# Linear attention and a gated feed-forward layer on one core: h split ahead of six splits, two sums a step sooner, casts a step later

## The chip, the cores and the metric

The kernel runs on one core of one Trainium2 chip. The metric is the device time in microseconds (us) of an execution, given as the median of several runs. The engines are named as the profile names them: PE is TensorE's matmuls and PEld its weight loads, DVE is VectorE, ACT ScalarE, POOL GpSimd and SP SyncE.

## What is computed

An attention without a score matrix is followed by a gated feed-forward layer (8 sequences of 576 tokens, 8 heads of 64; 4608 tokens of 512, 1536 hidden):

```python
q_s = softmax(q, axis=-1)               # over the 64 of a head
k_s = softmax(k, axis=2)                # over the 576 tokens
kv = np.einsum('bhsd,bhse->bhde', k_s, v)
x = np.einsum('bhsd,bhde->bhse', q_s, kv)   # then to 4608 x 512
gate = 1.0 / (1.0 + np.exp(-(x @ w_gate)))
return (gate * (x @ w_val)) @ w_out
```

## The kernel before

The tokens are worked through in nine windows of 512 (w = 0 to 8). Window 0 goes another way, in which the weights are also read and prepared; it ends some 180 us into the span. Each window from 1 on has six steps, `at` = 0 to 5, one for each pair of blocks of 128 hidden columns.

A step of window w is one call of `g1` and one of `g2`. `g1` makes gate and value of a pair of blocks by a Strassen scheme: seven products of 12 matmuls each (line 655), from c_hl (the activations, split into a rounded high part and the difference, fp32r) and the split weights a_w and s_sb. The first, third, fifth and seventh product go to the PSUM tile y, the second and sixth to z, the fourth to rr. The third accumulates onto the first, so `nc.scalar.copy(out=sg[:, 0], in_=y)` (line 673) has to read the first product before. Copies and additions (lines 675 to 687) combine them in sg, sigmoids (688, 691, 692) and multiplications (694 to 696) make the hidden values there. `h_split` (lines 705 and 706) splits these into h_hi and h_lo on VectorE, which reads sg for the last time. `g2` multiplies h of the step before with the output weights into acc (line 723, 24 matmuls); in a window's step 0 it is the last step of the window before, and `acc_out` copies acc to x_32 on ScalarE (line 629) and sends it out.

Beside window w the attention of window w + 1 is prepared, in pieces that `side_a` and `side_b` issue after `g1` and `g2` of a step:

- step 0: row maxima of q are taken and sent, q and two tiles of k have their maxima subtracted
- step 1: the rest of k, the exponentials of q and k (lines 457, 357), and the sums of exponentials of k^T (`k_sum`, line 313: an ACTIVATE with an accumulator on a kT tile, 128 x 576) for the third and fourth pair of heads
- step 2: the k-v products (`k_mm`, line 378); the subtraction on qT; `k_done`, which scales the k-v products into kmax_b (line 388) and, in `kv_split`, casts them to kv_sb on ScalarE (line 412) and takes the difference on VectorE (line 413)
- step 3: exponentials of qT; `k_sum` for the first two pairs of heads of the sequence after
- step 4: split of qT, the products with kv_sb that make x (`x_mm`, line 538), copies to x_32, and `c_subs`, the differences of activations that the next window's scheme needs
- step 5: ahead of h, the seven splits of `c_split` (casts on ScalarE, line 594; differences on VectorE, line 595); loads for the window after the next

Sequences exist for windows 2 to 7 only, so `k_sum`, `k_mm` and `k_done` run beside windows 1 to 6. The order on each engine is the order in which the code issues (a manual schedule): each engine works through its own list, and an instruction that waits holds what stands behind it.

Of the kernel before, what the change touches and what calls it, by code (L numbers as in the profile page):

```python
# [51 lines left out]
def attn_moe(ctx: ExitStack, tc: tile.TileContext, qf, qn, qT, k, kT, v, wg, wv, wo, out):  # L52
# [32 lines left out]
    kv_0 = f_last[:, 0].rearrange("p n (h e) -> p (n h) e", e=P)  # L85
# [225 lines left out]
    def k_sum(b, hp):  # L311
        t = kT_sb.pop((b, hp))
        nc.scalar.activation(
            t, t, AF.Exp, bias=kneg[b][:, hp:hp + 1], accum_out=ksum[b][:, hp:hp + 1]
        )
# [33 lines left out]
    def k_sub(b, t, eng=nc.vector):  # L349
        n = KTILES[t][1]  # L350
        kt = kt_sb[b, t]
        eng.tensor_tensor(out=kt[:n], in0=kt[:n], in1=kmb[b][:n], op=ALU.subtract)

    def k_exp(b, t):
        n = KTILES[t][1]
        kt = kt_sb[b, t]
        nc.scalar.activation(kt[:n], kt[:n], AF.Exp)
# [26 lines left out]
    def diag_put(o, ps, k_r, h0, h1):  # L384

        for a in range(2):
            sl = slice(a * D, (a + 1) * D)
            nc.vector.tensor_tensor(  # L388
                out=o(sl), in0=ps[sl, :, sl],
                in1=k_r[sl, h0:h1].unsqueeze(2).broadcast_to([D, h1 - h0, D]), op=ALU.mult,  # L390
            )
# [8 lines left out]
    def k_done(b):  # L400
        k_r = ksum.pop(b)
        nc.vector.tensor_scalar_add(k_r, k_r, EPS)
        nc.vector.reciprocal(k_r, k_r)
        kv = kmax_b[:, 0:NP * D].rearrange("p (h e) -> p h e", e=D)
        diag_put(lambda sl: kv[sl], kvps.pop(b), k_r, 0, NP)
        kv_split(b, lambda sl: kv[sl])

    def kv_split(b, kv):
        hi, lo = (kv_sb[:, b % 2, i] for i in range(2))
        for a in range(2):  # L410
            sl = slice(a * D, (a + 1) * D)
            nc.scalar.copy(out=hi[sl, :, sl], in_=kv(sl))  # L412
            nc.vector.tensor_tensor(
                out=lo[sl, :, sl], in0=kv(sl), in1=hi[sl, :, sl].bitcast(F32), op=ALU.subtract
            )
# [19 lines left out]
    def qn_send(w, what):  # L435
        t = (q_m if what == "m" else q_r)[w]
        row = dpool.tile([H * T], F32, name=f"q_{what}_row")
        nc.sync.dma_start(
            out=row.rearrange("(p i) -> p i", p=P), in_=t.rearrange("p i one -> p (i one)")
        )  # L440
        q_row[w, what] = row.rearrange("(h t) -> h t", t=T)

    def qn_max(w, c):
        if c == 0:
            q_m[w] = const.tile([P, NC * TI, 1], F32, name="q_m")
        nc.vector.tensor_reduce(
            out=q_m[w][:, c * TI:(c + 1) * TI], in_=qn_sb[w, c], axis=AX.X, op=ALU.max
        )

    def qn_sub(w, c, eng=nc.vector):  # L450
        t = qn_sb[w, c]
        m = q_m[w][:, c * TI:(c + 1) * TI]
        eng.tensor_tensor(out=t, in0=t, in1=m.broadcast_to([P, TI, D]), op=ALU.subtract)

    def qn_exp(w, c):
        t = qn_sb[w, c]
        nc.scalar.activation(t, t, AF.Exp)

    def qn_sum(w, c):
        t = qn_sb[w, c]  # L460
        if c == 0:
            q_r[w] = const.tile([P, NC * TI, 1], F32, name="q_r")
        nc.vector.tensor_reduce(
            out=q_r[w][:, c * TI:(c + 1) * TI], in_=t, axis=AX.X, op=ALU.add
        )
        if c == NC - 1:
            t = q_r[w]
            nc.vector.tensor_scalar_add(t, t, EPS)
            nc.vector.reciprocal(t, t)
            if w >= NF:  # L470
                qn_send(w, "r")
# [15 lines left out]
    def qT_sub(w, hp, eng=nc.vector):  # L487
        t = qT_sb[w, hp]
        eng.tensor_tensor(out=t, in0=t, in1=q_b.pop((w, "m", hp)), op=ALU.subtract)
# [12 lines left out]
    def qT_exp(w, hp):  # L502
        t = qT_sb[w, hp]
        nc.scalar.activation(t, t, AF.Exp)
# [65 lines left out]
    def quarter(kh, th):  # L570
        return x_32[:, 2 * kh:2 * kh + 2, th * HT:(th + 1) * HT]
# [15 lines left out]
    def c_split(i):  # L587
        if i % 2 == 0:
            t = cpool.tile([P, 2 if i < 6 else 1, 2, 2, HT], F32R, name="c_hl", tag=f"c{i // 2}")
            for x in range(i, min(i + 2, 7)):  # L590
                c_hl[x] = t[:, x % 2]
        src = c_32.pop(i) if i in c_32 else quarter(*{B11: (0, 0), B21: (1, 0), B22: (1, 1)}[i])
        hi, lo = (c_hl[i][:, x] for x in range(2))
        nc.scalar.copy(out=hi, in_=src)
        nc.vector.tensor_tensor(out=lo, in0=src, in1=hi.bitcast(F32), op=ALU.subtract)
# [104 lines left out]
    def h_split(w, p):  # L700
        h_hl[w, p] = hi, lo = [
            two.tile([P, 2, T], F32R, name="h", tag=f"h_{x}") for x in ("hi", "lo")
        ]
        hi, lo = (t.rearrange("p i (q t) -> p (i q) t", q=2) for t in (hi, lo))
        nc.vector.tensor_copy(out=hi, in_=sg[:, :, 0])
        nc.vector.tensor_tensor(  # L706
            out=lo, in0=sg[:, :, 0], in1=hi.bitcast(F32), op=ALU.subtract
        )
# [24 lines left out]
    def side_a(n, p):  # L733

        b = n if n < B else None
        if p == 0:
            for c in range(NC):
                qn_max(n, c)
            qn_send(n, "m")
            for c in range(NC):  # L740
                qn_sub(n, c)
            if b is not None:
                k_sub(b, 0); k_sub(b, 1)
        if p == 1:
            if b is not None:
                for t in range(2, 5):
                    k_sub(b, t)
            for c in range(NC):
                qn_exp(n, c)
            if b is not None:  # L750
                for t in range(5):
                    k_exp(b, t)
                k_sum(b, 2); k_sum(b, 3)
            for c in range(NC):
                qn_sum(n, c)
        if p == 2:
            if b is not None:
                for t in range(5):
                    k_mm(b, t)
            for hp in range(NP):  # L760
                qT_sub(n, hp)
            if b is not None:
                k_done(b)
        if p == 3:
            for hp in range(NP):
                qT_exp(n, hp)
        if p == 4:
            for hp in range(NP):
                qT_split(n, hp)
# [49 lines left out]
    def beside_first(j):  # L819
        if j == 6:  # L820
            k_done(1)
        if 7 <= j <= 10:
            x_ev(1, j - 7)
        if 6 <= j <= 9:
            qT_split(1, j - 6)
# [180 lines left out]
    for j in range(NJ):  # L1006
        g1_0(j)
        beside_first(j)
        split = splits.get(j)
        if split is not None:  # L1010
            split_hi(split)
        if j > 0:
            wo_hi(j - 1)
        if j + 2 < NJ:
            w_top(j + 2)
        if j + 1 < NJ:
            w_join(j + 1)
            wo_top(j + 1)
        wo_join(j)
        if j > 0:  # L1020
            g_mul_0(j - 1)
        if j + 3 < NJ:
            w_low(j + 3)
        if j + 2 < NJ:
            wo_low(j + 2)
        g_sig_0(j)
        if j > 0:
            wo_save(j - 1)
        if j + 3 < NJ:
            load_wo(j + 3)  # L1030
        if j + 5 < NJ - 1:
            load_w(j + 5)
        if j == 7:
            load_w(NJ - 1)
        if split is not None:
            split_lo(split)
        if j + 1 in splits:
            w_sums(splits[j + 1])
        if j > 0:
            g2_0(j - 1)  # L1040
        if j == 3:
            kv_split(0, lambda sl: kv_0[sl, :, sl])
        after_first(j)

    wo_hi(NJ - 1)
# [9 lines left out]
    for w in range(1, NW):  # L1055
        last = w == NW - 1
        for at in range(NS):
            p = step(w, at)
            end = last and at == NS - 1
            g1(w, p, None if end else step(w + (at + 1) // NS, (at + 1) % NS))  # L1060
            if at == NS - 1 and not last:
                for i in range(7):
                    c_split(i)
            h_split(w, p)
            if not last:
                side_a(w + 1, at)
            if prev is None:
                g2_0(NJ - 1)
                wo_next(1, 0)
                wo_next(1, 1)  # L1070
            else:
                g2(*prev)
                if not end:
                    wo_next(w + (at + 1) // NS, (at + 1) % NS)
            prev = (w, at)
            if not last:
                side_b(w + 1, at)
# [39 lines left out]
```

## Time and profile before

| | before |
|---|---|
| median of 3 runs | 982.61 us (979.5 to 984.96) |
| span of the profiled execution | 984.2 us, mean TensorE clock 0.985 of full speed |
| busy: PE, PEld | 954.0 us (97%), 824.0 us (84%) |
| busy: DVE, ACT, POOL | 613.1 us (62%), 471.4 us (48%), 167.3 us (17%) |
| mean share of the DMA engines, bytes | 262 GB/s, 257.78 MB |
| chain of work that ended last | PE 66%, DMA 17%, DVE 7%, ACT 7% |

The profiled execution lies inside the range of the runs, 1.6 us above their median. Busy time of an engine is summed over the whole span; what a step waits for is read from the timeline of that step. The clock is below full speed only in the first slices of the span.

### The profile page before, as it was taken

How to read it: one execution, taken by the hardware profiler on the slowest of the kernel's cores; microseconds unless marked ns; L12 is line 12 of the kernel's file. 1: busy time of each engine (PE TensorE's matmuls, PEld its weight loads, DVE VectorE, ACT ScalarE, POOL GpSimd, SP SyncE). 2: the span in 40 equal slices, each digit the busy share in tenths (PEclk: the TensorE clock that was granted, in tenths of full speed). 3: DMA queues.
4: the chain of work that ended last, by engine and by line, in shares of the span. 5: the costliest groups of instructions: out<-in, count | busy, mean ns of one | idle time of the engine just before them, and what ended most of it. 6: DMA issues, size and time to landing. Idle time of an engine off the chain costs nothing.

```text
span 984.2 us, 15634 instructions
## 1 busy us (share of the span) xinstructions
PE 954.0 (97%) x6062; PEld 824.0 (84%) x6062; DVE 613.1 (62%) x1013; ACT 471.4 (48%) x812; POOL 167.3 (17%) x316
## 2 busy tenths in 40 slices
PE   5899999799999999999999999999999999999998
PEld 5544544599999999999989999899999999999997
DVE  8688778776666566755684667557654655463242
ACT  4589785553436354525362545353434434533222
POOL 0110001221122112111111111121112121212210
PEclk7899999899999999999999999999999999999999
DMA  9987484899699978998899869996998779858662
GB/s 337 330 244 267 165 291 166 302 350 323 203 245 361 306 229 212 374 284 259 180 381 304 261 143 375 332 276 132 374 317 239 216 237 312 248 176 251 199 206 74
DMA packets 93864, 257.78 MB, mean 262 GB/s; under 512 B 15264, under 2 KB 17568, under 8 KB 93024
## 3 DMA queue, kind: packets, MB, share of 16 engines
q0 software_dynamic: 43712, 168.32, 56.9%
q1 hardware_dynamic: 50080, 88.48, 30.6%
q8 instruction: 48, 0.79, 0.4%
q14 instruction: 24, 0.20, 0.1%
HBM read 228.20 MB, written 28.56 MB: 261 GB/s over the span
## 4 chain that ended last, share of the span: by engine, by line
PE 66%; DMA 17%; DVE 7%; ACT 7%; issue 2%; SPq 1%; POOL 0%; DVEq 0%; ACTq 0%; POOLq 0%
PE gv L655 37%; PE acc L723 19%; DMA ring<-k_in 3%; DMA q_m_row<-q_m 3%; PE gv L610 3%; DMA q_b<-q_m_row 3%; DMA kmax_row<-k_max 2%; PE gv L538 2%; DMA ring<-qT_in 1%; PE at L378 1%; PE acc L637 1%; DMA ring<-qn_in 1%; DMA s<-s_sb 1%; DMA wo<-wo_hl 1%; PE at L538 1%
## 5 line engine op out<-in xcount | busy, mean ns | idle before, releaser
L655 PE MATMUL gv<-c_hl,s_sb 128*128 128x256 f32 x2304 | 288.1, 280 | 4.3 <-ACT sg L673 4.2
L655 PEld LDWEIGHTS gv<-c_hl,s_sb 128*128 128x128 f32 x2304 | 276.7, 188 | 6.9 <-ACT sg L673 6.5
L723 PE MATMUL acc<-wo_hl,h 128*128 128x512 f32 x1152 | 272.2, 392 | 0.0
L723 PEld LDWEIGHTS acc<-wo_hl,h 128*128 128x128 f32 x1152 | 213.1, 188 | 44.3
L655 PE MATMUL gv<-c_hl,a_w 128*128 128x256 f32 x1728 | 226.1, 279 | 0.7 <-DVE a_w L269 0.7
L655 PEld LDWEIGHTS gv<-c_hl,a_w 128*128 128x128 f32 x1728 | 214.9, 188 | 5.2 <-issue 1.0
L278 POOL DMA_DIRECT2D s_sb<-s x188 | 100.1, 532 | 321.8 <-PE gv L655 317.5
L681 DVE TENSOR_TENSOR sg<-gv,sg 128x512 f32<-128x512 f32 x48 | 33.2, 691 | 163.0 <-PE gv L655 163.0
L234 POOL DMA_DIRECT2D wo_hl<-wo x96 | 50.9, 531 | 297.6 <-PE acc L723 295.4
L683 ACT COPY sg<-gv 128x512 f32<-128x512 f32 x48 | 28.1, 586 | 106.4 <-PE gv L655 106.4
L610 PE MATMUL gv<-x,f_w 128*128 128x512 f32 x160 | 72.4, 606 | 5.5 <-ACT h L618 5.5
L673 ACT COPY sg<-gv 128x512 f32<-128x512 f32 x48 | 28.0, 583 | 89.8 <-PE gv L655 65.1
L685 DVE TENSOR_TENSOR sg<-sg 128x512 f32<-128x512 f32 x48 | 33.2, 692 | 58.9 <-ACT sg L683 58.9
L610 PEld LDWEIGHTS gv<-x,f_w 128*128 128x128 f32 x160 | 30.5, 194 | 43.7 <-issue 36.0
L706 DVE TENSOR_TENSOR h<-sg,h 128x1024 fp32r<-128x1024 f32 x48 | 58.8, 1226 | 1.6
L688 ACT ACTIVATE sg<-sg 128x512 f32<-128x512 f32 x48 | 30.3, 632 | 55.8 <-DVE sg L687 55.8
L694 DVE TENSOR_TENSOR sg<-sg 128x512 f32<-128x512 f32 x48 | 33.2, 693 | 33.5 <-ACT sg L688 33.5
L637 PE MATMUL acc<-wo_t,h 128*128 128x512 f32 x96 | 45.3, 617 | 5.7 <-DVE h L622 5.6
L678 ACT COPY sg<-gv 128x512 f32<-128x512 f32 x48 | 28.1, 586 | 44.7 <-PE gv L655 44.7
L637 PEld LDWEIGHTS acc<-wo_t,h 128*128 128x128 f32 x96 | 18.8, 199 | 30.0 <-issue 21.7
L675 ACT COPY sg<-gv 128x512 f32<-128x512 f32 x48 | 28.1, 586 | 26.2 <-PE gv L655 26.1
L412 ACT CAST kv_sb<-kmax_b 64x256 fp32r<-64x256 f32 x14 | 5.7, 404 | 67.1 <-DVE kmax_b L388 66.8
(152 smaller groups left out, 1054.8 us busy)
## 6 DMA issues: line engine op xcount, KB each, us to landing
s_sb<-s POOLq DMA_DIRECT2D x188, 512.0 KB, 7.6
wo_hl<-wo POOLq DMA_DIRECT2D x96, 512.0 KB, 6.0
s<-s_sb POOLq DMA_DIRECT2D x6, 2048.0 KB, 7.6
out<-x SPq DMA_DIRECT2D x36, 256.0 KB, 9.6
ring<-k_in SPq DMA_DIRECT2D x28, 256.0 KB, 15.0
ring<-qn_in SPq DMA_DIRECT2D x28, 256.0 KB, 10.3
q_b<-q_m_row SPq DMA_DIRECT2D x56, 128.0 KB, 8.6
ring<-qT_in SPq DMA_DIRECT2D x28, 256.0 KB, 8.9
```

The costliest lines, as they stand in the source:

```text
L234: nc.gpsimd.dma_start(out=t.rearrange("p h e -> p (h e)"), in_=wo_dram[2 * p + i].bitcast(F32R))
L278: nc.gpsimd.dma_start(out=s_sb[:, i].rearrange("p h n e -> p (h n e)"), in_=s_dram[p][:, i * n:(i + 1) * n].bitcast(F32R),)
L538: nc.tensor.matmul(ps[:, f:t], lhsT=kl if lh else kh, rhs=rh[:, f:t], start=(lh == 0 and rh is qh), stop=(lh == 1),)
L610: nc.tensor.matmul(ps[n], lhsT=w[:, kt // 2, sl], rhs=x_0[:, kt], start=(kt == 0), stop=(kt == NK - 1),)
L637: nc.tensor.matmul(acc[0][m], lhsT=h_0[j][:, m * P:(m + 1) * P], rhs=wo_t[j // 2][:, j % 2], start=(j == 0), stop=(j == NJ - 1),)
L655: nc.tensor.matmul(ps[:, n], lhsT=lh(kt), rhs=c_hl[i][:, x, kt], start=(first and n == 0 and kt == 0 and lh is wh and x == 0), stop=(last ...
L681: nc.vector.tensor_tensor(out=sg[:, 0], in0=rr, in1=sg[:, 0], op=ALU.add)
L685: nc.vector.tensor_tensor(out=sg[:, 3], in0=sg[:, 3], in1=sg[:, 2], op=ALU.add)
L688: nc.scalar.activation(sg[:, 0:2, 0], sg[:, 0:2, 0], AF.Sigmoid)
L694: tt(out=sg[:, 0:2, 0], in0=sg[:, 0:2, 0], in1=sg[:, 0:2, 1], op=ALU.mult)
L706: nc.vector.tensor_tensor(out=lo, in0=sg[:, :, 0], in1=hi.bitcast(F32), op=ALU.subtract)
L723: nc.tensor.matmul(acc[w][m], lhsT=h[lh][:, i, sl], rhs=o[i][:, rh], start=(at == 0 and i == 0 and lh == 0 and rh == 0), stop=(at == NS - ...
```

## The change

Three pieces of work are issued elsewhere; nothing is added to or taken from the computation, and no DMA changes its place on its queue.

- At the end of a window, `c_split(0)` stays first, then comes `h_split`, then the other six `c_split`.
- The two `k_sum` of step 1 are issued in step 0, after its subtractions.
- `kv_split` leaves `k_done` (step 2) and is issued at the start of step 3. In window 0 both stay together where they were.

```diff
         diag_put(lambda sl: kv[sl], kvps.pop(b), k_r, 0, NP)
-        kv_split(b, lambda sl: kv[sl])
-
-    def kv_split(b, kv):
+        kv_32[b] = lambda sl: kv[sl]
+
+    kv_32 = {}
+
+    def kv_split(b):
+        kv = kv_32.pop(b)
...
                 k_sub(b, 0); k_sub(b, 1)
+                k_sum(b, 2); k_sum(b, 3)
         if p == 1:
...
                 for t in range(5):
                     k_exp(b, t)
-                k_sum(b, 2); k_sum(b, 3)
...
         if p == 3:
+            if b is not None:
+                kv_split(b)
             for hp in range(NP):
                 qT_exp(n, hp)
...
             if at == NS - 1 and not last:
-                for i in range(7):
+                c_split(0)
+                h_split(w, p)
+                for i in range(1, 7):
                     c_split(i)
-            h_split(w, p)
+            else:
+                h_split(w, p)
```

The lists of the engines show the three moves. Line numbers of the changed kernel are 3 higher from line 413 on.

ScalarE, window 1, from the last sigmoids of step 0 to the first copy of step 1, in the kernel before (sg holds the products of g1, kt_106 and kt_107 are the kT tiles, x_101 is x_32):

```order
L691 ACTIVATE sg<-sg 128x256
L692 ACTIVATE sg<-gv 128x256
L629 COPY x_101<-acc 128x512 x4
L673 COPY sg<-gv 128x512
L675 COPY sg<-gv 128x512
```

The same stretch of this engine in the changed kernel:

```order
L694 ACTIVATE sg<-sg 128x256
L695 ACTIVATE sg<-gv 128x256
L313 ACT_TABLE_LOAD
L313 ACTIVATE kt_106,k_sum<-kt_106,k_neg 128x576
L313 ACTIVATE kt_107,k_sum<-kt_107,k_neg 128x576
L632 COPY x_101<-acc 128x512 x4
L676 COPY sg<-gv 128x512
L678 COPY sg<-gv 128x512
```

A table load and the two sums now stand ahead of the copies of acc.

ScalarE, from the end of step 1 of window 1 to the first copy of step 2, and on to the first table load of step 2, in the kernel before:

```order
L457 ACT_TABLE_LOAD
L457 ACTIVATE ring<-ring 128x512 x4
L357 ACTIVATE ring<-ring 128x512 x4
L357 ACTIVATE ring<-ring 64x512
L313 ACTIVATE kt_106,k_sum<-kt_106,k_neg 128x576
L313 ACTIVATE kt_107,k_sum<-kt_107,k_neg 128x576
L673 COPY sg<-gv 128x512
L675 COPY sg<-gv 128x512
L678 COPY sg<-gv 128x512
L683 COPY sg<-gv 128x512
L688 ACT_TABLE_LOAD
```

The same stretch of this engine in the changed kernel:

```order
L691 ACT_TABLE_LOAD
L691 ACTIVATE sg<-sg 128x2x256
L694 ACTIVATE sg<-sg 128x256
L695 ACTIVATE sg<-gv 128x256
L460 ACT_TABLE_LOAD
L460 ACTIVATE ring<-ring 128x512 x4
L357 ACTIVATE ring<-ring 128x512 x4
L357 ACTIVATE ring<-ring 64x512
L676 COPY sg<-gv 128x512
```

The copy follows the nine exponentials directly, and step 1's sigmoids have a table load of their own ahead of them. The list of ScalarE grows by 12 table loads over the program.

VectorE, from the last multiplication of a window's step 5 (window 1) to the first addition of the next window, in the kernel before (c_hl are the split activations, h the split hidden values):

```order
L696 TENSOR_TENSOR sg<-gv,sg 128x256
L595 TENSOR_TENSOR c_hl<-x_101,c_hl 128x512
L595 TENSOR_TENSOR c_hl<-ring,c_hl 128x512 x2
L595 TENSOR_TENSOR c_hl<-x_101,c_hl 128x512
L595 TENSOR_TENSOR c_hl<-ring,c_hl 128x512
L595 TENSOR_TENSOR c_hl<-x_101,c_hl 128x512
L595 TENSOR_TENSOR c_hl<-ring,c_hl 128x512
L705 CAST h<-sg 128x1024
L706 TENSOR_TENSOR h<-sg,h 128x1024
L681 TENSOR_TENSOR sg<-gv,sg 128x512
```

The same stretch of this engine in the changed kernel:

```order
L699 TENSOR_TENSOR sg<-gv,sg 128x256
L598 TENSOR_TENSOR c_hl<-x_101,c_hl 128x512
L708 CAST h<-sg 128x1024
L709 TENSOR_TENSOR h<-sg,h 128x1024
L598 TENSOR_TENSOR c_hl<-ring,c_hl 128x512 x2
L598 TENSOR_TENSOR c_hl<-x_101,c_hl 128x512
L598 TENSOR_TENSOR c_hl<-ring,c_hl 128x512
L598 TENSOR_TENSOR c_hl<-x_101,c_hl 128x512
L598 TENSOR_TENSOR c_hl<-ring,c_hl 128x512
L684 TENSOR_TENSOR sg<-gv,sg 128x512
```

The two instructions of h stand ahead of six of the seven differences.

## Rows read from the trace of the kernel before

In the rows of a timeline stand the start in us from the start of the span, the duration in us, engine, line, operation, out<-in, shapes and the count of merged instructions; in brackets the idle time before, and what ended it.

**Rows 1.** The page's first part, TensorE's busy time, share of the span, and instructions
```profile
PE 954.0 (97%) x6062; PEld 824.0 (84%) x6062; DVE 613.1 (62%) x1013; ACT 471.4 (48%) x812; POOL 167.3 (17%) x316
```

**Rows 2.** Waits of PE: releaser, us in all, times, longest
```profile
PE gv L655 <- ACT sg L673: 4.2, 9, 0.6
```

**Rows 3.** Timeline of PE, step 2 of window 2: start, us, [idle <- releaser]
```profile
312.14 1.52 PE L655 MATMUL gv<-c_hl,a_w 128*128 128x256 f32 x12
313.50 1.52 PE L655 MATMUL gv<-c_hl,s_sb 128*128 128x256 f32 x12
315.58 1.68 PE L655 MATMUL gv<-c_hl,s_sb 128*128 128x256 f32 x12 [0.55 <-ACT sg L673]
317.10 1.57 PE L655 MATMUL gv<-c_hl,a_w 128*128 128x256 f32 x12
318.51 2.99 PE L655 MATMUL gv<-c_hl,s_sb 128*128 128x256 f32 x24
```

**Rows 4.** Timeline of ACT, the same stretch
```profile
307.44 1.28 ACT L457 ACT_TABLE_LOAD   x1
308.74 2.20 ACT L457 ACTIVATE ring<-ring 128x512 f32<-128x512 f32 x4
...
313.45 0.76 ACT L313 ACTIVATE kt<-kt,k_neg 128x576 f32<-128x576 f32 x1
...
314.97 0.56 ACT L673 COPY sg<-gv 128x512 f32<-128x512 f32 x1
```

**Rows 5.** Timelines of ACT and of PE, step 3 of window 6
```profile
738.80 0.86 ACT L412 CAST kv_sb<-kmax_b 64x256 fp32r<-64x256 f32 x2 [11.74 <-DVE kmax_b L388]
...
740.33 1.68 PE L655 MATMUL gv<-c_hl,s_sb 128*128 128x256 f32 x12 [0.63 <-ACT sg L673]
```

**Rows 6.** Timelines of DVE and ACT, from window 3 to window 4
```profile
482.59 0.68 DVE L595 TENSOR_TENSOR c_hl<-ring,c_hl 128x512 fp32r<-128x512 f32 x1
483.19 0.68 DVE L705 CAST h<-sg 128x1024 fp32r<-128x1024 f32 x1
483.90 1.23 DVE L706 TENSOR_TENSOR h<-sg,h 128x1024 fp32r<-128x1024 f32 x1
...
485.22 0.58 ACT L673 COPY sg<-gv 128x512 f32<-128x512 f32 x1 [3.34 <-DVE h L706]
```

**Rows 7.** Timeline of PE, second and third product of step 0, windows 2, 8
```profile
283.02 3.34 PE L655 MATMUL gv<-c_hl,s_sb 128*128 128x256 f32 x24
...
883.76 3.12 PE L655 MATMUL gv<-c_hl,s_sb 128*128 128x256 f32 x24
```

**Rows 8.** Windows: busy us per engine (instructions), TensorE clock, DMA share, GB/s
```profile
753.00:762.52 9.52, 9.52 (x85) 9.51 (x84) 2.51 (x4) 4.05 (x6) 2.65 (x5) 1.00 0.72 215
802.67:812.56 9.89, 9.89 (x85) 9.89 (x84) 4.88 (x8) 3.52 (x7) 2.64 (x5) 1.00 0.97 297
```

**Rows 9.** Timeline of ACT, step 0 of window 2 and what follows
```profile
292.05 0.37 ACT L692 ACTIVATE sg<-gv 128x256 f32<-128x256 f32 x1
295.27 2.65 ACT L629 COPY x<-acc 128x512 f32<-128x512 f32 x4 [2.86 <-PE acc L723]
298.69 0.58 ACT L673 COPY sg<-gv 128x512 f32<-128x512 f32 x1 [0.77 <-PE gv L655]
```

**Rows 10.** Timeline of ACT, step 0 of window 1 and what follows
```profile
193.30 0.36 ACT L692 ACTIVATE sg<-gv 128x256 f32<-128x256 f32 x1
...
197.99 0.58 ACT L673 COPY sg<-gv 128x512 f32<-128x512 f32 x1 [0.83 <-PE gv L655]
```

**Rows 11.** Timeline of PE, second and third product of step 1, window 1
```profile
197.79 2.99 PE L655 MATMUL gv<-c_hl,s_sb 128*128 128x256 f32 x24
```

**Rows 12.** Timeline of ACT, sigmoid behind a table load, window 1, step 2
```profile
221.90 0.63 ACT L688 ACTIVATE sg<-sg 128x512 f32<-128x512 f32 x1 [0.33 <-DVE sg L687]
```

**Rows 13.** Timeline of ACT, step 4 of window 1
```profile
249.34 0.58 ACT L673 COPY sg<-gv 128x512 f32<-128x512 f32 x1 [1.26 <-PE gv L655]
```

**Rows 14.** Timeline of DVE, step 5 of window 1: k_neg written
```profile
271.25 0.15 DVE L307 TENSOR_SCALAR k_neg<-k_max 128x1 f32<-128x1 f32 x1
```

More of the change, by code (lines that the diff above doesn't have):

```diff
@@ L821, in beside_first @@
             k_done(1)
+            kv_split(1)
         if 7 <= j <= 10:
@@ L1041, in attn_moe @@
         if j == 3:
-            kv_split(0, lambda sl: kv_0[sl, :, sl])
+            kv_32[0] = lambda sl: kv_0[sl, :, sl]
+            kv_split(0)
         after_first(j)
```

## The prediction, made before the changed kernel ran

> **What bounds the kernel now.** I read the page's engine shares first: TensorE is busy 97% of the span [rows 1], so only what lets its matmuls start sooner or follow each other more closely can shorten it. The view of waits, for TensorE alone, comes next: from 206 us on the one thing it is seen to wait for is the ScalarE copy of line 673, nine times, 4.2 us in all [rows 2]. That copy moves the first product of a gate-value block from PSUM to sg, and the third product may not begin before it, as it accumulates into the same PSUM tile. The timelines then say why the copy is late. There are three places; I number a window's six steps 0 to 5, as the code's `at` does.
>
> Step 2, six windows (w 1 to 6). The reader should see that the products start 1.36 us apart (312.14, 313.50), while the third starts only at 315.58: 0.72 us late. Restarting costs a little more: that product takes 1.52 us up to the next, where the one behind it takes 1.41. So a wait shown as 0.55 us of idle costs 0.83, which is 0.28 more than its idle time [rows 3]. ScalarE was at work without a break: table load, nine exponentials, the two sums of exponentials of line 313 (313.45 to 314.97), and only then the copy [rows 4]. The two sums are 1.52 us of it.
>
> Step 3. ScalarE stands 11.74 us at the cast of line 412, until VectorE has written kmax_b; the copy queued behind it then holds TensorE for 0.63 us [rows 5]. This is the longest of three such waits.
>
> Step 0, seven windows. VectorE finishes its seven splits of c_hl, and only then the two halves of h; the copy of line 673 overwrites sg, which the second half reads, and so stands idle for 3.34 us [rows 6]. For TensorE this is nearly covered: two products that take 2.99 us undisturbed [rows 3] take 3.34 at 283.02 and 3.12 at 883.76, the first and the last of seven, most of them 0.11 to 0.13 long [rows 7]. These are too short to be listed as waits.
>
> Beside waits there is a pace. Two steps with no idle time, both at a granted clock of 1.00, which is 2.4 GHz, take 9.52 and 9.89 us for the same 84 matmuls, and TensorE's weight loads cover both without a gap [rows 8]. Some 12 of the 48 steps, counting parts, have the short spacing. In the PE timeline it holds until something interrupts it, the products of x always leave the long one behind, and it returns mostly in the step after a wait.
>
> **The change, part by part.** *Sums a step sooner.* Two ACTIVATEs leave step 1's chain and stand in step 0, between that step's last sigmoid and the four copies of acc. In step 2 the copy of line 673 can then start 1.52 us sooner by ScalarE's queue, where 0.72 is wanted; it now waits for its own product instead. All six waits go; they are priced below with the three of step 3.
>
> What it adds: sigmoids follow in step 1, so there is one table load for the exponentials and one back for the sigmoids, 12 more in all. In step 0 the sigmoid of line 692 ends at 292.42, the load takes 1.28 and the sums 1.52, so the copies could start at 295.2; they start at 295.27 today, because they wait for acc [rows 4, 9]. Cost nothing, hidden by the matmuls into acc; without that cover, 2.8 us a window. Behind them the copy of line 673 had 0.77 us of idle time before it [rows 9]. One window is tighter: in window 1 acc comes from shorter work, the sigmoid ends at 193.66 and the copy of line 673 started at 197.99 [rows 10]. There the sums end at 196.5; the four copies then run back to back until 198.7, if they take the 2.20 us of four ACTIVATEs of their size [rows 4], the copy of 0.58 ends at 199.3, and the third product was due at 199.2, 1.41 us into the row of two products [rows 3, 11]. I take 0.1 us, once; the ends are 0 and, if the copies take the 2.65 of a row in which they wait for acc [rows 9], 0.6 us. The load back to sigmoids follows the copy of line 683, where the first sigmoid waits for VectorE anyway: in a step that has such a load today, 0.33 us of that wait is still left after it [rows 12]. Cost nothing.
>
> Here the Trainium skill speaks against the change. Its page "ScalarE: Activation LUTs", section "What ACT_TABLE_LOAD costs", counts a drain of about 1.38 us beside the load of 1.28, 2.66 us for a switch. The load of 1.28 agrees with this trace; the drain does not show, since the exponentials start 1.30 us after the load does [rows 4]. By that page of the Trainium skill my sum would lose a little more than it does in the second rival below, about 4.6 us.
>
> *Casts a step later.* ScalarE no longer stands at kmax_b in step 2 with step 3's copy behind it. The casts (0.86 us) and their two differences on VectorE stand in step 3, when kmax_b has long been written; ScalarE's exponentials there end 0.86 us later, and the next copy had 1.26 us to spare [rows 13]. The result is needed by the products of x at the end of step 4. Three waits go. The nine of both edits are 4.2 us of idle and 9 x 0.28 = 2.5 us of restarts: 6.7 us.
>
> *h ahead of six splits.* No instruction is added. h is finished six splits sooner, some 3.6 us at 0.60 each (482.59 to 483.19) [rows 6], more than the 3.34 us for which the copy stood. The splits come 1.9 us later (h's two halves), and the next is first read one product after step 0 begins; the first split stays where it was. The seven waits of 0.35, 0.13 and five between or near them are 1.2 us. No DMA is moved on any queue by any of the three edits. Two later k loads of line 331 reuse buffers that those splits read, but are issued after them anyway.
>
> *Pace.* Nothing in the trace of before prices this. Bounds: every step at the long spacing costs 12 x 0.37 = 4.4 us; twice as many steps at the short one give 4.4. I look at each stretch of short spacing: about six and a half steps have it after a wait that goes away, and about two would keep it because no wait breaks it. I take a loss of 4.3 steps at 0.37, 1.6 us, nearer to the first bound because most returns followed a wait.
>
> Sum: 6.7 + 1.2 = 7.9 us less wait; less 0.1 and 1.6 leaves 6.2 us. The profiled execution spans 984.2 us and would come to 978.0. It lies 1.6 us above the median of the three runs, 982.61, from which I predict **976.4 us**.
>
> **The rivals.**
> *All at the long spacing.* Waits go as above, but without them nothing brings the short spacing back: 982.6 - 7.8 + 4.4 = 979.2, no change that can be told (0.5%, 4.9 us, is about what a measurement of this kernel can tell). For it: all steps after 771 us, where waits are fewest, have the long one. Against: it also came back behind the k-v products, with no wait. Its opposite, the short spacing kept because nothing interrupts it, gives 982.6 - 7.8 - 4.4 = 970.4.
>
> *The table switch costs more than its row.* If each of the added switches held ScalarE for the length of its load once more, 1.28 us [rows 4], the sigmoid of step 1 would come 1.28 - 0.33 = 0.95 us late [rows 12], and with it the exponentials of that step. Of the 1.52 us won there 0.57 would be left, against 0.72 wanted: 0.15 and 0.28 us in each of six windows, 2.6, and 1.3 in window 1, where nothing is to spare. That makes 976.4 + 3.9 = 980.3. The row of the load, with work 1.30 us after its start, speaks against it. The drain that the Trainium skill counts in "ScalarE: Activation LUTs" would do the same with 1.38 us; the trace has no room for it.
>
> *Slower: the sums hold the queue of ScalarE.* They now stand ahead of the copies of acc and of step 1's first copy. If one had to wait for its operands in step 0, everything behind it would wait too: past the 0.77 us of idle [rows 9] and about 0.5 us until the third product is due, each microsecond costs six. It decides from 2.6 us on (1.27 + 7.8/6, the pace aside); held 4 us it would cost 6 x 2.73 = 16.4 us, less 6.2: about 993. Against: their last operand, k_neg, is written at 271.25, 21 us ahead [rows 14].
>
> **How the numbers follow.** Forecast 0.50 (its own range 973.5 to 979), long spacing throughout 0.20, short spacing kept 0.16, dearer switch 0.10, slower 0.04. Range 971 to 981: it takes in the long spacing and the dearer switch, and leaves out the slower case and half of the 970.4 case. Faster by over 0.5% means below 977.7: three quarters of the forecast, the short spacing, and a fifth of the long spacing and the dearer switch: 0.375 + 0.16 + 0.06, 0.60. Slower 0.04. The rest, 0.36, is the same.
>
> **What would show it.** The view of TensorE's waits should list no wait for the copy of line 673 (676 in the new numbering) in steps 2 and 3; the ScalarE row of the copy in step 0 should be released by TensorE, not by h; the cast should show no idle time before it. Twelve more table loads of 1.28 us should be followed at once by their ACTIVATE. If those waits are gone and the time is 979 or more, the PE timeline should show steps of 9.89 us nearly throughout. Waits that remain in step 2, or a copy of acc that starts late in step 0, would prove me wrong.

## The result, and the profile after

The changed kernel took 974.73 us (median of 6 runs, 971.43 to 975.62); the kernel before, beside it, 982.73 us (6 runs, 979.5 to 986.03). The ratio is 0.9906, interval [0.9887, 0.9925]: 8.0 us faster, where 6.2 were forecast. On another chip it was 974.85 against 980.87 us, ratio 0.9937 [0.9917, 0.9956], 6.0 us. The forecast of 976.4 us and its range held.

The page's first part of the changed kernel answers to [rows 1]:

```profile
PE 946.6 (97%) x6062; PEld 819.3 (84%) x6062; DVE 613.2 (63%) x1013; ACT 488.3 (50%) x824; POOL 168.3 (17%) x316
```

ScalarE has 12 instructions more, the table loads, and is busy for 16.9 us more; TensorE is busy for less time with the same 6062 matmuls.

TensorE's waits in the changed kernel (releaser, us in all, times, longest):

```profile
PE gv L658 <- DVE a_w L269: 0.7, 1, 0.7
...
PE gv L658 <- DMA s_sb<-s: 0.3, 1, 0.3
```

The copy, line 676 now, is no longer among them; [rows 2] had it nine times. From 200 us on the view lists no wait of TensorE at all. The timeline of ScalarE in windows 1, 2 and 6 says why (start, duration; in brackets the idle time before, and what ended it):

```profile
192.04 2.03 ACT L632 COPY x<-acc 128x512 f32<-128x512 f32 x4
193.94 0.61 ACT L676 COPY sg<-gv 128x512 f32<-128x512 f32 x1
...
278.95 0.59 ACT L676 COPY sg<-gv 128x512 f32<-128x512 f32 x1 [2.75 <-PE gv L658]
...
287.97 1.28 ACT L313 ACT_TABLE_LOAD   x1
289.27 0.78 ACT L313 ACTIVATE kt<-kt,k_neg 128x576 f32<-128x576 f32 x1
...
290.87 2.65 ACT L632 COPY x<-acc 128x512 f32<-128x512 f32 x4
...
306.76 2.70 ACT L357 ACTIVATE ring<-ring 128x512 f32<-128x512 f32 x5
309.73 0.59 ACT L676 COPY sg<-gv 128x512 f32<-128x512 f32 x1 [0.27 <-PE gv L658]
...
315.98 1.28 ACT L691 ACT_TABLE_LOAD   x1
317.52 0.63 ACT L691 ACTIVATE sg<-sg 128x512 f32<-128x512 f32 x1 [0.25 <-DVE sg L690]
...
727.17 0.59 ACT L676 COPY sg<-gv 128x512 f32<-128x512 f32 x1 [11.21 <-PE gv L658]
...
736.07 0.82 ACT L415 CAST kv_sb<-kmax_b 64x256 fp32r<-64x256 f32 x2
```

In step 2 the copy now has 0.27 us of idle time before it and is released by its own product (309.73), where ScalarE was at work without a break in [rows 4]. In step 3, where ScalarE stood 11.74 us at the cast in [rows 5], it now stands 11.21 us at the copy, and TensorE releases it; the cast follows the sigmoids, without a wait. In step 0 the copy (278.95) waits for TensorE, where it waited for h in [rows 6]. The sums fit ahead of the copies of acc (290.87), and one step later the sigmoid that has the new load ahead of it (317.52) still waits 0.25 us for VectorE.

TensorE in the changed kernel, products of steps 1 (window 1), 0 and 2 (window 2), for [rows 11, 7, 3]:

```profile
193.33 1.57 PE L658 MATMUL gv<-c_hl,s_sb 128*128 128x256 f32 x12
195.18 1.65 PE L658 MATMUL gv<-c_hl,s_sb 128*128 128x256 f32 x12 [0.27 <-DMA s_sb<-s]
...
278.75 2.99 PE L658 MATMUL gv<-c_hl,s_sb 128*128 128x256 f32 x24
...
309.53 2.99 PE L658 MATMUL gv<-c_hl,s_sb 128*128 128x256 f32 x24
```

Second and third product run into each other in 2.99 us in steps 0 and 2. The wait of 0.27 us in window 1 is new and is not the copy's: that one ended at 194.55 (193.94 + 0.61), 0.19 us before the third product was due (193.33 + 1.41). The row names a transfer of weights, and a second profile of the same kernel lacks the wait (below).

**Counting waits and pace.** I took the starts of the matmuls of g1 from the traces (e8 and e12, which have 14 and 8 matmuls more, are not in the table). Neighbours within a step start either about 113.3 ns apart or about 117.8 ns (12 of them make 1.36 and 1.41 us, the two products of [rows 3] among them); where a spacing is clearly longer, what it has above 117.8 ns is counted as wait (in e1, e4 and e7 some of it is a lower clock behind a wait, see the end). All from the start of step 1 of window 1 to the end of the span; "left" is the stretch less the waits and less 4.5 ns for each long spacing. Apart from those three places the granted clock is 1.00 in every one of these stretches, up to the last two microseconds of the span. Ahead of them it is not: in the kernel before it was last at its lower level from 173.8 to 180.6 us, so not only in the first slices of the span.

| kernel | step 1 of window 1 starts | from there to the end | waits | long spacings | left |
|---|---|---|---|---|---|
| before | 195.98 | 788.3 | 8.7 | 2836 | 766.8 |
| changed | 191.51 | 780.7 | 1.1 | 2899 | 766.6 |
| changed, again (e9) | 193.21 | 779.8 | 0.6 | 2817 | 766.5 |
| sums alone (e1) | 194.40 | 791.5 | 12.3 | 2704 | 767.0 |
| casts alone (e2) | 193.34 | 785.4 | 7.9 | 2370 | 766.8 |
| h alone (e3) | 193.97 | 790.5 | 7.3 | 3625 | 766.9 |
| sums and h (e4) | 193.08 | 787.9 | 13.7 | 1663 | 766.7 |
| sums and casts (e5) | 191.94 | 780.1 | 1.6 | 2614 | 766.7 |
| sums and casts, again (e10) | 193.87 | 779.4 | 1.7 | 2426 | 766.8 |
| casts and h (e6) | 191.70 | 788.8 | 4.5 | 3884 | 766.8 |
| longer hold (e7) | 194.24 | 788.3 | 9.7 | 2636 | 766.7 |
| two matmuls more (e11) | 193.90 | 776.3 | 0.7 | 1986 | 766.7 |

What is left is the same within 0.5 us: **from there on, these kernels differ in waits and spacing and in nothing else that adds up to more than that.** From before to changed, the stretch is 7.5 us shorter, 7.6 of it waits; the spacing gave and took 0.3. The other 4.5 us between the two spans lie ahead of it, in window 0 and the first step, and vary from execution to execution (191.5 to 196.0 over these profiles).

### The profile page after: what moved, and what is told of

Read it like the earlier page. It is cut to its first block, busy times and chain, and to the rows that moved or that the text cites. A ratio compares the mean times of both kernels' runs of the same rounds, so it can differ in the third digit from the quotient of the medians.

```text
span 972.2 us, 15629 instructions
## 1 busy us (share of the span) xinstructions
PE 946.6 (97%) x6062; PEld 819.3 (84%) x6062; DVE 613.2 (63%) x1013; ACT 488.3 (50%) x824; POOL 168.3 (17%) x316
## 4 chain that ended last, share of the span: by engine, by line
PE 91%; DMA 3%; DVE 2%; ACT 2%; issue 1%; POOL 0%; SPq 0%; POOLq 0%; DVEq 0%; ACTq 0%
PE gv L658 48%; PE acc L726 27%; PE gv L613 6%; PE at L378 3%; PE acc L640 3%; PE gv L541 2%; DMA kmax_row<-k_max 1%; DMA s<-s_sb 1%; PE at L541 1%; DMA s_sb<-s 1%; DMA lent<-k_in 1%; ACT s_sb L265 0%; PE acc L564 0%; ACT f_w L162 0%; DVE a_w L269 0%
## 5 line engine op out<-in xcount | busy, mean ns | idle before, releaser
L658 PE MATMUL gv<-c_hl,s_sb 128*128 128x256 f32 x2304 | 284.6, 279 | 0.3 <-DMA s_sb<-s 0.3
L234 POOL DMA_DIRECT2D wo_hl<-wo x96 | 51.1, 533 | 297.4 <-PE acc L726 297.3
L492 DVE TENSOR_TENSOR ring<-ring,q_b 128x512 f32<-128x512 f32 x28 | 18.6, 691 | 34.9 <-DMA ring<-qT_in 34.8
```

What stands on the lines that cost most here:

```text
L234: nc.gpsimd.dma_start(out=t.rearrange("p h e -> p (h e)"), in_=wo_dram[2 * p + i].bitcast(F32R))
L658: nc.tensor.matmul(ps[:, n], lhsT=lh(kt), rhs=c_hl[i][:, x, kt], start=(first and n == 0 and kt == 0 and lh is wh and x == 0), stop=(last ...
```

## The experiments

First, the parts one by one on one chip. The additive theory (A): each edit takes away its own waits. The give-back theory (B): the casts stand behind kmax_b, which is written when transfers allow it, so that a step won before it is waited for there. The kernel before took 985.21 us on that chip (35 runs).

**Sums alone (e1).**

```diff
@@ p == 0
                 k_sub(b, 0); k_sub(b, 1)
+                k_sum(b, 2); k_sum(b, 3)
@@ p == 1
-                k_sum(b, 2); k_sum(b, 3)
```

> Only the two sums move (step 1 to step 0); h and the casts stand as before. Theory A (the parts add, as the prediction's sum has it): the six waits of step 2 go, about 4.7 us, the three of step 3 stay at about 2 us, a new wait of 0.5 us in window 1; about 978.5 for 982.7 before. Theory B (the casts' place limits what the sums give): the time at which kmax_b is written is set by transfers that start at the end of the window before, not by TensorE, so TensorE reaches step 3 about 0.8 us sooner and waits there 0.8 us longer in five or six windows; the waits of step 3 grow from about 2 us to 6 or 7, and the time is 981.5 to 983.5, no difference that can be told. The list of TensorE's waits tells them apart: for the copy of line 673, A three waits of about 1.1 us of idle in all, B five or six with 4 us or more.

Measured: 986.97 us, ratio 1.0017 [0.9987, 1.0046]. The six waits of step 2 are gone, and those of step 3 grew. Waits of TensorE, and timelines of ScalarE, VectorE and TensorE in step 3 of window 3, in this run:

```profile
PE gv L655 <- ACT sg L673: 7.7, 5, 2.1
```
```profile
435.94 0.86 ACT L412 CAST kv_sb<-kmax_b 64x256 fp32r<-64x256 f32 x2 [13.21 <-DVE kmax_b L388]
436.83 0.59 ACT L673 COPY sg<-gv 128x512 f32<-128x512 f32 x1
```
```profile
432.39 2.71 DVE L489 TENSOR_TENSOR ring<-ring,q_b 128x512 f32<-128x512 f32 x4 [6.85 <-DMA ring<-qT_in]
...
435.49 0.88 DVE L388 TENSOR_TENSOR kmax_b<-at,k_sum 64x256 f32<-64x256 f32 x2
```
```profile
437.46 1.70 PE L655 MATMUL gv<-c_hl,s_sb 128*128 128x256 f32 x12 [2.14 <-ACT sg L673]
438.98 2.75 PE L655 MATMUL gv<-c_hl,a_w 128*128 128x256 f32 x12
441.53 3.38 PE L655 MATMUL gv<-c_hl,s_sb 128*128 128x256 f32 x24
```

Read them from the right end back: TensorE waits 2.14 us for the copy, the copy stands behind the cast, the cast waits for kmax_b, and ahead of kmax_b VectorE waited 6.85 us for qT to land. And kmax_b does not come sooner because TensorE does. Counted from the first product of a window, step 3 of windows 2 to 6 starts at 51.5 to 51.8 us in the kernel before and at 50.4 to 51.2 in e1, while kmax_b is written at 52.9 to 54.0 us and at 53.5 to 55.0. In the changed kernel step 3 starts at 49.9 to 51.1 and kmax_b is written at 53.4 to 54.1, but nothing of ScalarE stands behind it there. Theory A falls, B holds.

**Casts alone (e2).**

```diff
-        kv_split(b, lambda sl: kv[sl])
+        kv_32[b] = lambda sl: kv[sl]
@@ p == 3
+            if b is not None:
+                kv_split(b)
```

> Only the casts move (step 2 to step 3). Both theories: the three waits of step 3 (1.1 us of idle, 2 us with restarts) go, the six of step 2 (3.1 us of idle) and the small ones of step 0 stay; about 980.7 for 982.7 before, if the spacing of the matmuls stays as it is. A theory in which ScalarE's later exponentials in step 3 cost something would show waits for the copy of line 673 in step 4.

Measured: 982.19 us, 0.9963 [0.994, 0.9985]. Its waits of TensorE:

```profile
PE gv L658 <- ACT sg L676: 4.4, 6, 2.0
```

The waits of step 3 are gone, six of step 2 stay, one of 2.0 us among them. This is the only single edit that gains. By the table its stretch is 2.9 us shorter than that of the kernel before, but only 0.8 us of this are waits; 2.1 are spacing (466 long ones fewer).

**h alone (e3).**

```diff
-                for i in range(7):
+                c_split(0)
+                h_split(w, p)
+                for i in range(1, 7):
                     c_split(i)
-            h_split(w, p)
+            else:
+                h_split(w, p)
```

> Only h moves ahead of six splits. Theory A: the seven short waits of step 0 (1.2 us together) go, 981.5 for 982.7 before. Theory B: of those 1.2 us a part comes back as longer waits in step 3, 0.1 us in each window; 981.5 to 982.7. Both: the ScalarE copy of line 673 in step 0 waits for TensorE and no longer for h.

Measured: 987.18 us, 1.0015 [0.9991, 1.0039]. The waits of step 0 are gone (waits 8.7 to 7.3 us in the table), but nearly all steps have the long spacing in this profile: 789 long ones more, 3.6 us.

**Sums and h, casts where they were (e4):** both of the diffs above.

> The changed kernel with the casts back in step 2 (sums and h moved). Theory A: 974.7 plus the 2 us of step 3's waits, about 977. Theory B: in the changed kernel kmax_b is written 2.0, 2.4, 2.4, 4.1, 2.6 and 4.2 us after step 3 begins in windows 1 to 6; with cast and copy behind it the third product would wait from 0.3 to 2.5 us in each, 8 us with restarts, so 981 to 983, most of the gain gone. TensorE's waits for the copy of line 673: A about 1.5 us of idle, B 5 us or more.

Measured: 987.12 us, 1.0011 [0.9984, 1.0038]. Waits of TensorE in this run:

```profile
PE gv L655 <- ACT sg L673: 9.6, 6, 2.4
```

Two edits that take away the waits of steps 2 and 0 gain nothing as long as the casts hold the copy of step 3: in all the waits are 5.0 us longer than in the kernel before. The profiled execution, 982.74 us, is one of the fastest of the twelve, and by the table it had 5.3 us back by spacing.

For the second set, on a chip on which the kernel before took 980.31 us, the table gave a third theory (C): the time is waits plus spacing, and what an edit is worth is the sum of both, whichever edit it is.

**Changed kernel without the h edit (e5):** seven splits, then h, as before.

> The changed kernel with h back behind the seven splits (sums and casts moved). Theory A (only waits count): the waits of steps 2 and 3 stay away, the short ones of step 0 come back, 1.2 us; 0.1% above the changed kernel, 0.8% below before. Theory C (waits and the spacing of the matmuls count, each short-spaced matmul being 4.5 ns shorter): the same 1.2 us, but the interruptions of step 0 also bring the short spacing back in some windows; with a fifth to a half of the matmuls at the short spacing against a quarter in the changed kernel the time lies between 4 us below and 2 us above it, and span and count of short spacings in the profile agree with the sum of the two terms within 1 us from the first matmul of window 1 on.

Measured: 973.42 us, 0.9938 [0.9923, 0.9953]. The short waits of step 0 came back (about 0.12 us each, the last 0.28), and the profile has 285 long spacings fewer, 1.3 us: no loss by the table. Whether there is one in time is for e10, which stands beside the changed kernel on one chip.

**Changed kernel with the sums back in step 1 (e6).**

> The changed kernel with the two sums back in step 1 (h and casts moved). The six waits of step 2 come back, about 3.1 us of idle and 4.8 us in all; the waits of steps 0 and 3 stay away, and the 0.5 us of window 1 is saved. About 4.3 us above the changed kernel, so 0.5% below before (additive for this pair, since the casts are out of the way). If casts and sums did not depend on each other, it would also differ from before by just the 2 us of step 3 and the 1.2 us of step 0, 0.3%.

Measured: 979.8 us, 0.9997 [0.9982, 1.0012]. Waits of TensorE, and its timeline in step 2 of window 2:

```profile
PE gv L658 <- ACT sg L676: 2.3, 6, 0.4
```
```profile
310.22 1.57 PE L658 MATMUL gv<-c_hl,s_sb 128*128 128x256 f32 x12
312.18 1.68 PE L658 MATMUL gv<-c_hl,s_sb 128*128 128x256 f32 x12 [0.40 <-ACT sg L676]
313.71 1.57 PE L658 MATMUL gv<-c_hl,a_w 128*128 128x256 f32 x12
```

The product ahead of the wait and the one behind the restarted product take 1.57 us as listed, the long spacing, and so everywhere: 3884 long spacings, none short. Waits fell by 4.2 us and the spacing took 4.7. So the time is that of the kernel before, where 0.5% less had been expected. The rival "all at the long spacing" happened, only in another kernel.

**A longer hold in step 0 (e7)** measures the slack behind the sums: two ACTIVATEs of one element, each with a table load.

```diff
                 k_sum(b, 2); k_sum(b, 3)
+                nc.scalar.activation(pad_a[:, 0:1], pad_a[:, 1:2], AF.Sigmoid)
+                nc.scalar.activation(pad_a[:, 2:3], pad_a[:, 3:4], AF.Exp)
```

> The changed kernel with two one-element ACTIVATEs behind the sums of step 0, a sigmoid and an exponential, which force two more table loads there in each of six windows (the outputs are not used). Theory of the rows (a switch costs its load of 1.28 us and nothing more): ScalarE is held about 3 us longer in step 0, the copies of acc start 3 us later, the copy of line 676 in step 1 ends 1.5 to 2 us after the third product is due, and TensorE waits there in six windows, about 12 us in all. Theory of a drain (2.66 us for a switch): the hold is 5.7 us and the waits 4.5 us each, 27 us in all. The ScalarE timeline of step 0 shows the gap between a load and the ACTIVATE behind it: about 0.01 us by the rows, 1.4 us by the drain. A wait over 2 us may also show the clock at its lower level behind it, as in e4.

Measured, one execution: 984.28 us. ScalarE and TensorE in window 2:

```profile
297.90 1.28 ACT L749 ACT_TABLE_LOAD   x1
299.20 0.20 ACT L749 ACTIVATE pad_a<-pad_a 128x1 f32<-128x1 f32 x1
299.40 1.28 ACT L750 ACT_TABLE_LOAD   x1
300.70 0.20 ACT L750 ACTIVATE pad_a<-pad_a 128x1 f32<-128x1 f32 x1
300.81 2.03 ACT L633 COPY x<-acc 128x512 f32<-128x512 f32 x4
```
```profile
303.38 1.68 PE L659 MATMUL gv<-c_hl,s_sb 128*128 128x256 f32 x12 [0.66 <-ACT sg L677]
```

A switch holds ScalarE for 1.28 us, and work starts 1.30 us after it did: no drain. Loads and ACTIVATEs hold the engine for 2.9 us (297.90 to 300.81), of which TensorE loses 0.92 in each of windows 2 to 6, where 1.5 to 2 had been expected; so about 2.0 us of slack were there, not the 1.27 of the prediction. The 0.6 us by which the copies of acc shrink (2.65 to 2.03, no more waiting for acc in between) are what I had left out.

**Moving the spacing (e8, e11, e12).** If the spacing depends on how matmuls fall, more matmuls of odd sizes should turn it. In front of the first product of a step:

```diff
+        if extra:
+            nc.tensor.matmul(
+                y[:, 0, 0:extra], lhsT=wa(A11)(0)[0](0), rhs=c_hl[B11][:, 0, 0, 0:extra],
+                start=True, stop=False, skip_group_check=True,
+            )
```

> The changed kernel with one extra matmul ahead of the first product of some steps, of 32 to 256 columns, on the same weights and into the PSUM tile that the first product then overwrites: in step 5 of windows 1, 2, 4, 6, 7, in steps 0 to 3 of window 7 and in steps 0 to 4 of window 8. It asks what brings the short spacing back. If it is the idle time of a wait, a matmul more does nothing and windows 7 and 8 stay at the long spacing throughout. If it is where a matmul falls against its weight load, a matmul of another length can set it as well as a wait can, and some of the steps behind an insertion turn to the short spacing (9.52 us a step) and stay there until the next insertion or interruption. Each extra matmul costs about 0.1 us, 1.5 us in all.

Measured, one execution: 977.33 us, with sizes of 32 to 256 columns in 14 steps. In windows 7 and 8 one step became short, behind a 256-column one in window 7, with no idle time near it; the others stayed long. In windows 2 to 4 two steps became short and six long, so that there are 10 short steps in all. The next runs put a 64-column matmul into step 0 and a 256-column one into step 1 of window 7 (e11), or that and 64 columns in step 5 of windows 1 to 6 (e12), beside the changed kernel (e9) and the one without the h edit (e10), all on one chip (before: 980.87 us, 16 runs).

> The changed kernel once more, on the same chip as the three runs beside it. If the spacing of TensorE's matmuls is fixed by the order of the work, its profile shows again 11 to 13 steps of some 9.5 us, in the same steps as in the first profile of the changed kernel; if chance sets it in each execution, the short spacing stands in other steps, and their number differs by more than 3. Time 0.988 to 0.993 of the kernel before.

Measured: 974.85 us (972.75 to 976.21), 0.9937 [0.9917, 0.9956]. Its profile has 13 short steps to the first one's 12, and from step 5 of window 1 on they are the same steps; only in window 1 did they move, where the first profile had waited for weights. This one did not:

```profile
193.21 1.98 PE L658 MATMUL gv<-c_hl,a_w 128*128 128x256 f32 x12
195.02 2.99 PE L658 MATMUL gv<-c_hl,s_sb 128*128 128x256 f32 x24
```

> The changed kernel with h behind the seven splits again, beside the changed kernel on one chip. By the sum of the prediction it is 1.2 us slower than that kernel (seven short waits of step 0 come back). By the theory of waits and spacing it is within 0.3% of it and not sure to be slower, since its seven waits of 0.12 us (1.2 us with the one of window 8) come with three more steps of the short spacing (3 x 0.37 = 1.1 us).

Measured: 974.86 us, 0.9936 [0.9912, 0.9959], the time of the changed kernel to 0.01 us. Waits are 1.1 us longer, the spacing 1.8 us better. The h edit is worth nothing that can be told; the 1.2 us forecast for it are within what these runs leave open, but in the traces the spacing outweighs them.

> The changed kernel with two more matmuls in window 7, of 64 columns ahead of the first product of step 0 and of 256 columns ahead of that of step 1; they write where the first product writes next, with its start, so the output is unchanged. If the way in which matmuls fall sets the spacing, the steps of windows 7 and 8 behind them show 9.5 us in place of 9.9: up to 10 steps x 0.37 = 3.7 us, 0.2 us for the two matmuls, so 3 to 3.5 us less than the changed kernel. If idle time alone brings the short spacing, nothing turns, and the time is that of the changed kernel within 1 us.

Measured: 971.66 us (969.48 to 972.45), 0.9903 [0.9878, 0.9928]; every run is below every run of the changed kernel beside it. First products of two neighbouring steps of window 7, and a stretch with the granted clock (third figure from the right), in e9:

```profile
807.04 1.58 PE L658 MATMUL gv<-c_hl,a_w 128*128 128x256 f32 x12
...
822.43 1.58 PE L658 MATMUL gv<-c_hl,a_w 128*128 128x256 f32 x12
```
```profile
838.02:847.95 9.93, 9.93 (x86) 9.89 (x85) 2.38 (x5) 4.36 (x7) 2.66 (x5) 1.00 0.69 208
```

and in e11:

```profile
807.99 1.52 PE L658 MATMUL gv<-c_hl,a_w 128*128 128x256 f32 x12
...
823.01 1.52 PE L658 MATMUL gv<-c_hl,a_w 128*128 128x256 f32 x12
```
```profile
838.02:847.95 9.93, 9.93 (x87) 9.89 (x86) 2.75 (x5) 4.47 (x8) 2.66 (x5) 1.00 0.72 217
```

The step is 15.02 us long in place of 15.39, at the same clock of 1.00, and so are all ten steps from there to the end: 3.7 us, less 0.2 for the two matmuls; 3.2 measured. This version is faster than both kernels.

> As the run before, and with a matmul of 64 columns ahead of the first product of step 5 in each of windows 1 to 6. If the way in which matmuls fall sets the spacing, more of the steps 5 to 2 of those windows are short (up to 3 steps x 0.37 us more in each of six windows, 6 us), so 3 to 9 us less than the changed kernel. If idle time alone brings the short spacing, no more steps are short than in the changed kernel, and the time is the same within 1 us.

Measured: 972.9 us (971.45 to 977.02), 0.9926 [0.9899, 0.9953]. Window 7 turned as in e11. In windows 2 to 4 the short spacing stands in other steps than in e11, and windows 1 to 6 have 12 in place of 13. That is 2.0 us less than the changed kernel, where 3 to 9 had been expected, and no gain over e11. So the spacing can be moved, and cannot yet be steered.

## Why the prediction was right, and where it was not

**The waits** were the mechanism, and their term had the right size: 7.9 us forecast (6.7 and 1.2), 7.6 and 8.1 us gone in the two profiles of the changed kernel. Copy released by its product in step 2, by TensorE in step 3, cast without a wait: the marks that I had named are there.

**What I took apart, I priced wrongly.** I gave the sums the six waits of step 2, the casts the three of step 3, h the seven of step 0, as if they added. They don't: sums alone, h alone, and both together are the kernel before within their intervals, and without the sums the other two are as well (e6). The two edits that matter need each other, and the table's waits say so most plainly: 8.7 us before, 12.3 with the sums, 7.9 with the casts, 1.6 and 1.7 with both. The reason is that kmax_b is written when qT has landed: whoever reaches step 3 sooner waits there longer, unless the casts are out of the way. The sum held because the change makes both; as the working took each edit by itself, that is luck. That I did not follow the gain of step 2 to the next place where it could be waited for is the gap in the working: I looked at step 3 as a wait of its own.

**Table loads and window 1.** "Cost nothing" holds: the sigmoid still waits for VectorE after the new load. By the Trainium skill ("ScalarE: Activation LUTs", "What ACT_TABLE_LOAD costs") a drain should have followed; the rows of e7 with two switches in a row have none. The 0.1 us taken for window 1 was 0: the four copies took 2.03 us, less than my 2.20.

**Pace** is the term that was mis-sized: a loss of 1.6 us was taken, and the traces show +0.3 and -0.1 us (63 long spacings more in one profile, 19 fewer in the other, against one profile of the kernel before). The working does not show how 4.3 steps come out of the six and a half and the two that it names. That short spacing comes back after a wait and goes at an interruption was a pattern of this one trace. The changed kernel, almost without waits, has 12 and 13 short steps, as many as before; e6, with six waits, has none. Without this term the sum is 7.8 us, and 974.8 us the time. That the gains on the two chips, 8.0 and 6.0 us, lie on either side of 6.2 says nothing for the term.

**The rivals.** The slower one did not occur, and its threshold was too low: with some 2.0 us of slack in place of 1.27 it decides from about 3.3 us on (2.0 + 7.8/6). The profiled execution of before lies further above the median than I said: around a span there are 1.8 us (974.03 for the changed kernel's 972.2), so its 984.2 stand for some 986.0, the time of the slowest run (986.03), 3.4 us above 982.61 and not 1.6; as the gain was taken off the median, this cost nothing.

**Open:** what sets the spacing of back-to-back matmuls. Shown is that it is not the clock, that two added matmuls turned it (e11), and that neither a wait nor a lack of one decides it alone. The order of the matmuls does not decide it alone either: the kernel without the h edit had 15 short steps in one profile (e5) and 17 in the other (e10), and all of window 8 was long in the first and nearly all of it short in the second. So a difference in spacing between two single profiles is not yet what an edit is worth.

## What to carry to other kernels

Follow a gained stretch to the next instruction that waits for something which does not move with it, a transfer above all: if the engine there holds work of the bounding engine behind that wait, the gain is given back, and the two edits are worth something only together. Take single edits apart in runs before you credit them, and count waits and matmul spacing in the trace apart from each other; here the two explain all of the difference between twelve profiles from step 1 of window 1 on. An edit that removes short waits can be worth nothing where the spacing comes out worse with it.

## What the runs showed of the hardware

Back-to-back matmuls of one shape had two steady spacings at the same granted clock of 1.00, 113.3 and 117.8 ns, 4% apart; one matmul of 64 and one of 256 columns changed it for the next ten steps.

Behind three waits of 2.1 to 2.7 us TensorE's clock was lower. Windows around the 2.14-us wait of e1, and around one of 2.10 us in e4 (third figure from the right is the granted clock):

```profile
434.00:437.30 3.30, 1.32 (x12) 1.11 (x10) 3.01 (x8) 1.28 (x3) 0.53 (x1) 1.00 1.12 311
437.50:442.50 5.00, 5.00 (x29) 5.00 (x30) 2.19 (x5) 0.99 (x2) 0.54 (x1) 0.66 1.24 245
442.60:445.00 2.40, 2.40 (x23) 2.40 (x22) 0.74 (x2) 0.59 (x1) 0.53 (x1) 1.00 1.11 242
```
```profile
536.10:539.60 3.50, 3.50 (x17) 3.50 (x18) 1.51 (x4) 0.97 (x2) 0.20 (x1) 0.52 1.21 256
539.70:545.00 5.30, 5.30 (x47) 5.25 (x46) 2.14 (x4) 1.32 (x3) 1.30 (x3) 1.00 1.12 242
...
738.00:742.00 4.00, 1.62 (x14) 1.42 (x13) 3.10 (x8) 1.88 (x4) 0.54 (x1) 1.00 1.10 299
```

Behind these two waits TensorE ran at 0.66 and 0.52 on the mean, mostly at its lower level of 1.2 GHz; behind the wait of 2.72 us in window 1 of e7 it was at 0.50 from 201.8 to 205.1 us; in e1 the second product behind the wait took 2.55 us up to the next (438.98 to 441.53), where 1.36 or 1.41 is usual. Other waits of this length were not followed by it: 1.97 us in e2, 1.99 in e1, and 2.38 in e4, which ended at 741.53; there the clock is 1.00 from 741.5 to 746.0 us as well, and the products behind it start 1.51 and 1.42 us apart. What decides between them is open. So a wait that grows can cost more than its length, which my price per wait (idle time and 0.28 us) did not have.
